# Recurrence blocks back inside the hidden products, and a changed start: a wider table of decays, zero products sooner, and the second batch's inputs on ScalarE's queue

## The chip, the cores and the metric

The kernel runs on one core of a Trainium2 chip. The core has five engines with a queue each: TensorE (PE, matmuls; PEld is its weight load), VectorE (DVE), ScalarE (ACT), GpSimd (POOL) and SyncE (SP, which only issues transfers here). The metric is the device time of one execution in microseconds. Before the change the median of three runs is 671.96 us (670.41 to 673.58).

## The reference

Two stages. The first is a retention recurrence over 4 batches, 8 heads, 768 tokens and 64 dimensions, with a decay `gamma` per head:

```
state = gamma * state + k_t (outer) v_t
y_t   = (1/8) * q_t @ state
```

The second takes the 3072 x 512 matrix of all `y` (tokens by heads and dimensions) through a two-layer network: `h = x @ w_in` (512 to 2048), `g = max(0.01 h, h)`, `out = g @ w_out` (2048 to 512). The weights arrive as 64-bit floats and are turned into 32-bit floats on the core.

## The kernel before

**The recurrence in chunks.** The 768 tokens are six chunks (c = 0 to 5) of 128. In a chunk, a batch b needs four groups of small matmuls: `score` (keys times queries, 16 matmuls on 64 x 64 tiles of the array), `reads` (queries times the state carried in, 8 on 64 x 64 tiles), `values` (masked scores times decayed values, 8 on 128 x 64 tiles) and `state` (keys times values, 8 on 128 x 64 tiles). Between `score` and `values`, DVE multiplies the scores by a triangular mask (`masked`), and some engine multiplies the values by decays (`decay_v`: on GpSimd unless another is given). After `values` and `state`, DVE takes the tokens into `x` (`tokens_taken`) and updates the state (`state_taken`, two operations of 256 columns).

**The network.** It goes by chunk and by unit u (four units of 512 hidden columns). Each matrix product is done with seven half-size products in place of eight, `seven`: M1, M6, M5, M4, M2, M7, M3 in the order `ORDER`, each of four 128 x 128 by 128 x 256 matmuls per unit (recorded as 8), into the PSUM banks A, B, C, D (M1 and M2 share A, M6 and M7 share B, M5 and M3 share C). `hidden` (L530 to L563) makes `g` from `x` and the differences `t` of `x`; `output` (L565 to L619) makes the result from `g` and its differences `gd`. Behind each product the engines take its bank: ScalarE copies M1 and M5 out (L540, L546), DVE does the sums (L446), ScalarE the leaky step (L535, L550). M1 and M2 use only `x`; M6, M5 and M4 use `t`. The order `FIRST` does M2 straight after M1.

**Order.** There is no scheduler: each engine does its instructions in the order in which the program emits them. `seven` is a generator that yields after each product, and `run(steps, at)` emits other work at chosen steps. Chunks 0 and 1 go together, unit by unit, while weights are still converted; chunks 2 to 5 follow one by one, with units in pairs: hidden, hidden, output of the pair.

**Visits.** From chunk 2 on the recurrence work of a later chunk stands behind an output (L843 to L858). A `visit(c, b, following)` (L310 to L344) handles batches b and b+1: scores of the first following batch into two single banks of tag "ff" (`score_apart`), reads, values, scores of the second following batch, states; DVE's masks, tokens, the four differences of `x` if the chunk is then complete, state updates; and then the loads of the next chunk's inputs. The queries and keys of batches 2 and 3 are loaded into the tile of an output not in use (`ahead`, L270). After a visit that completes a chunk, the first hidden goes in the order `FIRST`. Exceptions: in the last output of chunk 0, the scores of batches 0 and 1 of chunk 2 stand after M1 and a visit without following after M4 (L836); in the last output of chunk 1 the scores of batches 2 and 3 stand after M2 (L840).

**The start.** SyncE issues the transfers in order: queries and keys of batch 0 (`load_qk`), values of batch 0 (`load_v`), the same of batch 1, two weight pieces, and so on (L672 to L687). ScalarE issues one, the table of decays (L671): 8 rows of 780 columns. DVE sets the mask and then 256 columns of zeros (L688, L700). PE does seven products of zeros (`keep_busy`, L703), scores of batch 0, three matmuls that spread the decays over all partitions (L717 to L723, contraction over the table's 8 rows), scores of batch 1, values of batch 0, and so on until the first direct product of weights (`direct`, L522 at L739). DVE copies gains and carry `gk`, `gc` out of PSUM (L722) and multiplies batch 0's values (L726); ScalarE copies `gq` (L725). Each weight piece needs three ScalarE steps (`powers`, L419 to L422) and three DVE steps (`mantissas_upper` L431, `mantissas_rest` L440 and L442).

Of the kernel before, what the change touches and what calls it, by code (L numbers as in the profile page):

```python
# [18 lines left out]
C = 128  # L19
# [4 lines left out]
def kernel(  # L24
# [104 lines left out]

    def load_qk(c, b):  # L130
        nc.sync.dma_start(out=heads[c, b][0], in_=qk[c, b])

    def load_v(c, b):
        nc.sync.dma_start(out=heads[c, b][1][:, 1], in_=kv[c, b][:, 1])

# [31 lines left out]

    turn = [0]

    def new_am(c, b):  # L170

        i = turn[0]
        turn[0] = (i + 1) % (3 if (c, b) >= (2, 2) else 2)
        if i < 2:
            return work.tile([128, 2, HP, C], FP32, tag=f"am{i}", name=f"am_{c}_{b}")
        place = new_t(1, f"am_{c}_{b}").rearrange("p i k n -> p (i k n)")[:, 0 : 2 * HP * C]
        return place.rearrange("p (j a t) -> p j a t", j=2, a=HP)

    def new_t(c, name):
        return work.tile([128, 3, 2, N], FP32, tag=f"t{int(c == 1)}", name=name)  # L180

    def new_o(c, name="o"):
        return work.tile([128, 4, 2, N], FP32, tag=f"o{int(c > 0)}", name=f"{name}_{c}")

    def masked(c, b):
        am = new_am(c, b)
        nc.vector.tensor_tensor(
            out=am.rearrange("p j a t -> p (j a) t"),
            in0=scores[c, b].rearrange("p j a t -> p (j a) t"),
            in1=mask.unsqueeze(1).to_broadcast([128, H, C]), op=ALU.mult)  # L190
        scores[c, b] = am
# [25 lines left out]
    def state(c, b):  # L217
        y = heads[c, b][1]
        sp = for_state(sums_at[c, b])
        for a in range(HP) if c < NC - 1 else ():  # L220
            sums_of(sp, y, a)
# [47 lines left out]

    def ahead(c, b):  # L270


        if c >= NC:
            return
        if b < 2:
            x = work.tile([128, 2, HP, C], FP32, tag="qk", bufs=AHEAD, name=f"qk_{c}_{b}")
        else:
            if b == 2:
                room[c] = new_o(0).rearrange("p i k n -> p (i k n)")
            x = room[c][:, ds((b - 2) * 2 * HP * C, 2 * HP * C)]  # L280
            x = x.rearrange("p (s a t) -> p s a t", s=2, a=HP)
        heads[c, b] = [x, None]
        load_qk(c, b)

    def load_kv(c, b):
        y = work.tile([128, 2, H, D], FP32, tag="kv", bufs=AHEAD, name=f"kv_{c}_{b}")
        heads[c, b][1] = y
        nc.sync.dma_start(out=y, in_=kv[c, b])

    room = {}  # L290

    def score_apart(c, b):

        x = heads[c, b][0]
        ps = scores[c, b] = [psum.tile([128, HP, C], FP32, tag="ff", bufs=4, name=f"ap{j}_{c}_{b}")
                             for j in range(2)]
        for a in range(HP):
            for u in range(2):
                for j in range(2):
                    nc.tensor.matmul(ps[j][ts(u, 64), a, :], lhsT=x[ts(j, 64), 1, a, ts(u, 64)],  # L300
                                     rhs=x[ts(j, 64), 0, a, :])

    def masked_apart(c, b):
        am = new_am(c, b)
        for j, ps in enumerate(scores[c, b]):
            nc.vector.tensor_tensor(out=am[:, j], in0=ps,
                                    in1=mask.unsqueeze(1).to_broadcast([128, HP, C]), op=ALU.mult)
        scores[c, b] = am

    def visit(c, b, following=None, complete=False):  # L310

        bs, xb = (b, b + 1), xs[c][0]
        more = [(following[0], following[1] + i) for i in range(2)] if following else [None, None]
        early, late = more

        def do(f, at):
            if at is not None:
                f(*at)

        do(score_apart, early)  # L320
        for i in bs:
            reads(c, i)
        do(masked_apart, early)
        for i in bs:
            values(c, i)
        do(score_apart, late)
        for i in bs:
            state(c, i)
        do(masked_apart, late)
        for i in bs:  # L330
            tokens_taken(c, i, xb)
        if complete:
            if xs[c][1] is None:
                xs[c][1] = new_t(c, f"t_{c}")
            differences(*xs[c])
        for i in bs:
            state_taken(c, i)
        for i in bs:
            if c + 1 < NC:
                ahead(c + 1, i)  # L340
        for at in more:
            do(load_kv, at)
        for at in more:
            do(decay_v, at)  # L344

# [129 lines left out]
    ORDER = (0, 1, 2, 3, 4, 5, 6)  # L475
    FIRST = (0, 4, 1, 2, 3, 5, 6)

# [147 lines left out]
    def new_x(c):  # L625
        x = tile_x(c)
        return [x, new_t(c, f"t_{c}") if c < 3 else None]

# [15 lines left out]
    def scored(c, b):  # L644
# [4 lines left out]
        return do  # L649

    def differ(c):
        return lambda: differences(*xs[c])
# [11 lines left out]
    place_for(0, 1)  # L664
    place_for(0, 2, new_o(0, "in"))
    place_for(0, 3, new_o(1, "in"))
    words = tile_x("words").rearrange("p i k n -> p (i k n)")[:, 0 : 2 * W]
    xs = {0: new_x(0)}
    x, t = xs[0]
    rows = t[0:H, 1:3].rearrange("p i k n -> p (i k n)")[:, 0 : decay.shape[1]]  # L670
    nc.scalar.dma_start(out=rows, in_=decay)  # L671
    load_qk(0, 0)  # L672
    load_v(0, 0)
    load_qk(0, 1)
    load_v(0, 1)
    load_piece(0)
# [21 lines left out]

    nothing = t[:, 0, 0, :].bitcast(BF16)
    nc.vector.memset(t[:, 0, 0, :], 0.0)  # L700
    idle = psum.tile([128, 2, N], FP32, tag="ff", bufs=4, name="idle")

    def keep_busy(n):  # L703
        for _ in range(n):
            nc.tensor.matmul(idle.rearrange("p i n -> p (i n)"), lhsT=nothing[:, 0:128],
                             rhs=nothing, start=True, stop=True, skip_group_check=True)

# [6 lines left out]
    by_head, ones, place, g_q, g_c = (rows[:, i:j] for i, j in zip(ends, ends[1:]))  # L714
    keep_busy(7)
    score(0, 0)
# [4 lines left out]
    masked(0, 0)  # L721
    nc.vector.tensor_copy(out=dec[:, n_gq:], in_=tables[:, 0, 0 : H + HP])  # L722
    nc.tensor.matmul(spread.rearrange("p i n -> p (i n)"), lhsT=place, rhs=g_q, start=True,  # L723
                     stop=True, skip_group_check=True)
    nc.scalar.copy(out=dec[:, 0:n_gq], in_=spread.rearrange("p i n -> p (i n)"))  # L725
    decay_v(0, 0, nc.vector)  # L726
    score(0, 1)
# [75 lines left out]
    scored_later(3)  # L803
    later = hidden(1, 0, x1, t1, *parts[1][1:], order=FIRST)
    next(later)
# [14 lines left out]
    for u in range(NU):  # L820
        for c in range(2) if u > 0 else ():
            if c == 0:
                parts = []
            parts.append(new_g(c, u))
            run(hidden(c, u, *xs[c], *parts[c][1:]), rounds(1, 3))
        for c in range(2):
            if u == 0:
                os[c] = new_o(c)
            at = rounds(1, 4) if u < NU - 1 else {}
            if u == 0 and c == 0:  # L830
                put(at, s2=[differ(0)])
            if u == NU - 1 and NC > 2:
                if c == 0:
                    xs[2] = new_x(2)
                if c == 0:
                    at = {0: [scored(2, 0), scored(2, 1)], 3: [lambda: visit(2, 0)]}  # L836
                else:
                    at = {1: [lambda: ahead(2, 2), lambda: ahead(2, 3)],
                          2: [lambda: load_kv(2, 2), lambda: load_kv(2, 3)],
                          4: [scored(2, 2), scored(2, 3)]}  # L840
            run(output(c, os[c], [parts[c]], u == 0, u == NU - 1), at)

    if NC > 2:  # L843
        visit(2, 2, (3, 0) if NC > 3 else None, complete=True)
    for c in range(2, NC):
        os[c] = new_o(c)
        for p in range(NU // 2):
            pair = []
            for u in (2 * p, 2 * p + 1):
                pair.append(new_g(c, u))  # L850
                run(hidden(c, u, *xs[c], *pair[-1][1:], order=ORDER if u else FIRST), {})
            run(output(c, os[c], pair, p == 0, p == NU // 2 - 1), {})

            if c + 1 < NC and p == 0:
                xs[c + 1] = new_x(c + 1)
                visit(c + 1, 0, (c + 1, 2))
            elif c + 1 < NC and p == NU // 2 - 1:
                visit(c + 1, 2, (c + 2, 0) if c + 2 < NC else None, complete=True)  # L858

# [4 lines left out]
def _decay(H, D):  # L864
# [11 lines left out]
    place = np.concatenate([place, np.zeros((H - 2, place.shape[1]))])  # L876
    return np.concatenate([np.exp(-lg[:, None] * t[None, :]), np.eye(H), place],
                          axis=1).astype(np.float32)

# [62 lines left out]
```

## Time and profile before

| What | Value |
|---|---|
| median of three runs | 671.96 us |
| the profiled execution's own time | 671.96 us |
| its span, first to last instruction | 669.9 us |
| mean granted TensorE clock | 0.997 |
| PE busy | 661.1 us (99%) |
| DVE, ACT, POOL busy | 369.3, 176.2, 18.9 us |
| bytes read and written | 41.97 MB, 6.29 MB |

How to read the profile's lines. A line of a timeline gives start and duration in us, the engine, the line in the code, the operation, what it writes and reads by the program's names, shapes and how many records are merged; in brackets the idle time before it and what ended it. Durations of matmuls overlap: what a group costs is read from start to start. A line of waits gives who waited for whom, the total in us, how often, and the longest. A line by windows gives a stretch, its length, the busy share of each engine with the number of instructions, the granted TensorE clock (1.00 is full), the share of the transfer engines in use and the rate in GB/s.

### The profile page before, as it was taken

What the parts mean: (1) busy time and instruction counts of PE and PEld (TensorE: products, weight loads), DVE (VectorE), ACT (ScalarE), POOL (GpSimd) and SP (SyncE); (2) the same over time, 40 slices, a digit from 0 to 9 for tenths busy, and PEclk for the clock granted to TensorE, in tenths of its full rate; (3) what the DMA queues carried; (4) which work ended last, traced back from release to release, by engine and by line L of the source; (5) the groups of instructions that cost most, each with busy time, mean ns of one, the idle gap of its engine ahead of it and who ended that gap; (6) DMA issues with size and microseconds to landing.
All of it is one profiled execution on the core that took longest, in us unless ns stands there. A gap on an engine that the chain in (4) does not pass through costs nothing.

```text
span 669.9 us, 10441 instructions
## 1 busy us (share of the span) xinstructions
PE 661.1 (99%) x4503; PEld 573.7 (86%) x4505; DVE 369.3 (55%) x582; ACT 176.2 (26%) x322; POOL 18.9 (3%) x22
## 2 busy tenths in 40 slices
PE   8999999999999999999999999999999999999998
PEld 5888888888888888888888888888888888888886
DVE  4789969889888673344436413536433443541342
ACT  4764555264261002202102211300210210221210
POOL 0000000000000020001001001001000100000000
PEclk8999999999999999999999999999999999999999
DMA  8920311312322540020022003005001001000001
GB/s 329 393 100 32 125 64 66 124 64 103 117 79 90 221 179 1 0 100 28 1 90 100 1 0 127 1 6 184 1 0 52 13 1 64 0 1 1 0 1 63
DMA packets 15757, 48.92 MB, mean 73 GB/s; under 512 B 1752, under 2 KB 2008, under 8 KB 15712
## 3 DMA queue, kind: packets, MB, share of 16 engines
q1 hardware_dynamic: 15696, 48.24, 19.8%
q8 instruction: 35, 0.57, 0.3%
q14 instruction: 10, 0.08, 0.0%
q10 hardware_dynamic: 16, 0.02, 0.0%
HBM read 41.97 MB, written 6.29 MB: 72 GB/s over the span
## 4 chain that ended last, share of the span: by engine, by line
PE 98%; DMA 1%; DVE 0%; ACT 0%; issue 0%; SPq 0%; DVEq 0%
PE B_o L500 12%; PE A_o L500 12%; PE C_o L500 12%; PE A_h L500 12%; PE B_h L500 12%; PE C_h L500 12%; PE D_o L500 6%; PE D_h L500 6%; PE yp L210 4%; PE d L522 2%; PE ap L300 2%; PE ap L165 2%; PE yp L201 1%; PE yp L225 1%; DMA qk<-in_qk_dram 1%; ACT m L540 0%
## 5 line engine op out<-in xcount | busy, mean ns | idle before, releaser
L500 PE MATMUL A_h<-x,w 128*128 128x256 f32 x368 | 88.2, 382 | 2.7 <-ACT m L540 2.7
L500 PEld LDWEIGHTS A_h<-x,w 128*128 128x128 f32 x368 | 68.9, 190 | 14.1 <-ACT m L540 4.3
L500 PE MATMUL A_o<-g,w 128*128 128x256 f32 x288 | 68.0, 379 | 0.0
L446 DVE TENSOR_TENSOR m<-m,B_h 128x512 f32<-128x512 f32 x23 | 15.8, 686 | 90.6 <-PE B_h L500 90.6
L500 PEld LDWEIGHTS A_o<-g,w 128*128 128x128 f32 x288 | 54.7, 190 | 7.4
L535 ACT ACTIVATE g<-g 128x512 f32<-128x512 f32 x69 | 42.0, 630 | 72.7 <-DVE g L446 72.7
L540 ACT COPY m<-A_h 128x512 f32<-128x512 f32 x23 | 13.5, 586 | 176.6 <-PE A_h L500 156.3
L446 DVE TENSOR_TENSOR m<-m,B_o 128x512 f32<-128x512 f32 x16 | 11.0, 685 | 64.3 <-PE B_o L500 64.3
L500 PE MATMUL B_h<-t,w 128*128 128x256 f32 x184 | 43.5, 379 | 0.0
L500 PE MATMUL D_h<-t,w 128*128 128x256 f32 x184 | 43.5, 379 | 0.0
L500 PE MATMUL C_h<-t,w 128*128 128x256 f32 x184 | 43.5, 379 | 0.0
L500 PE MATMUL B_h<-x,w 128*128 128x256 f32 x184 | 43.5, 379 | 0.0
L500 PE MATMUL C_h<-x,w 128*128 128x256 f32 x184 | 43.5, 379 | 0.0
L500 PEld LDWEIGHTS B_h<-t,w 128*128 128x128 f32 x184 | 35.0, 190 | 4.8
L500 PEld LDWEIGHTS D_h<-t,w 128*128 128x128 f32 x184 | 35.0, 190 | 4.8
L500 PEld LDWEIGHTS B_h<-x,w 128*128 128x128 f32 x184 | 35.0, 190 | 4.8
L500 PEld LDWEIGHTS C_h<-x,w 128*128 128x128 f32 x184 | 35.0, 190 | 4.8
L500 PEld LDWEIGHTS C_h<-t,w 128*128 128x128 f32 x184 | 35.0, 190 | 4.8
L449 DVE TENSOR_TENSOR gd<-g,gd 128x512 f32<-128x512 f32 x48 | 33.2, 692 | 1.7
L500 PE MATMUL D_o<-gd,w 128*128 128x256 f32 x144 | 34.0, 379 | 0.0
L500 PE MATMUL C_o<-g,w 128*128 128x256 f32 x144 | 34.0, 379 | 0.0
L500 PE MATMUL B_o<-gd,w 128*128 128x256 f32 x144 | 34.0, 379 | 0.0
(122 smaller groups left out, 995.3 us busy)
## 6 DMA issues: line engine op xcount, KB each, us to landing
raw<-in_weights_dram SPq DMA_DIRECT2D x31, 512.0 KB, 4.1
kv<-in_kv_dram SPq DMA_DIRECT2D x17, 512.0 KB, 4.9
out_dram<-o SPq DMA_DIRECT2D x23, 256.0 KB, 2.2
qk<-in_qk_dram SPq DMA_DIRECT2D x11, 512.0 KB, 3.6
o<-in_qk_dram SPq DMA_DIRECT2D x8, 512.0 KB, 3.4
in<-in_qk_dram SPq DMA_DIRECT2D x5, 512.0 KB, 8.6
in<-in_kv_dram SPq DMA_DIRECT2D x3, 512.0 KB, 7.6
kv<-in_kv_dram SPq DMA_DIRECT2D x4, 256.0 KB, 7.0
```

The lines of the kernel that those rows point to most:

```text
L165: nc.tensor.matmul(ps[ts(u, 64), j, a, :], lhsT=x[ts(j, 64), 1, a, ts(u, 64)], rhs=x[ts(j, 64), 0, a, :])
L201: nc.tensor.matmul(ps[ts(i, 64), j, m, :], lhsT=st[b][ts(j, 64), a, :], rhs=x[ts(j, 64), 0, a, :], start=(m == 0), stop=False, skip_group_ ...
L210: nc.tensor.matmul(ps[ts(i, 64), j, m, :], lhsT=y[:, 1, 2 * a + j, :], rhs=am[:, j, a, :], start=(c == 0 and m == 0), stop=True, skip_grou ...
L225: nc.tensor.matmul(sp[ts(j, 64), a, :], lhsT=y[:, 0, 2 * a + j, :], rhs=y[:, 1, 2 * a + j, :], start=start, stop=True, skip_group_check=True)
L300: nc.tensor.matmul(ps[j][ts(u, 64), a, :], lhsT=x[ts(j, 64), 1, a, ts(u, 64)], rhs=x[ts(j, 64), 0, a, :])
L446: nc.vector.tensor_tensor(out=out, in0=a, in1=b, op=ALU.add)
L449: nc.vector.tensor_tensor(out=out, in0=a, in1=b, op=ALU.subtract)
L500: nc.tensor.matmul(half, lhsT=block(w, sa)[:, k, ts(i, 128)], rhs=rhs[:, k, :], start=(first and (i == 0 or split) and n == 0 and k == 0), ...
L522: nc.tensor.matmul(banks[r][:, i, :], lhsT=block(2 * u, r + 2 * kh)[:, k, ts(i, 128)], rhs=x[:, 2 * kh + th, k, :], start=(step == 0 and i ...
L535: nc.scalar.activation(g[:, i], g[:, i], AF.Prelu, alpha=0.01)
L540: nc.scalar.copy(out=got["m1"], in_=ps)
```

## The change

The visits go. From chunk 2 on the recurrence is emitted inside other products: the scores of two batches of chunk c+1 after M6 of the hidden product of units 0 and 2 of chunk c, and their reads, values and states after M2 of the same (`read`, `stage_y`); the differences of `x` after M6 of the chunk's last output. In the last outputs of chunks 0 and 1 the scores stand after M1 and the reads after M4; chunk 2's differences after M2 of chunk 1's. All hidden products of chunks 2 to 5 go in `ORDER`. Queries and keys of later chunks go to the two "qk" tiles, loaded when the tile before is read; scores always use the two-bank tiles of tag "att". The tags of the tiles `am`, `t` and `o` become plain rotations of two.

At the start: the table of decays has 32 rows (24 of them zeros), GpSimd sets the rows of the other partitions to zero, and the three spreading matmuls contract over 128 partitions. Zeros for `keep_busy` are 64 columns, set by DVE ahead of the mask, and read repeatedly; eight such products instead of seven. Batch 1's queries, keys and values are issued by ScalarE. Gains and carry are copied by ScalarE, and batch 0's values are multiplied by GpSimd.

```
-        nc.sync.dma_start(out=heads[c, b][0], in_=qk[c, b])
+    def load_qk(c, b, queue=nc.sync):
+        queue.dma_start(out=heads[c, b][0], in_=qk[c, b])
+    def load_v(c, b, queue=nc.sync):
+        queue.dma_start(out=heads[c, b][1][:, 1], in_=kv[c, b][:, 1])
...
-        am = new_am(c, b)
+        am = work.tile([128, 2, HP, C], FP32, tag="am", bufs=2, name=f"am_{c}_{b}")
...
-    def visit(c, b, following=None, complete=False):
...
+    def stage_y(c, bs, xb):
+        products(c, bs)
+        for b in bs:
+            taken(c, b, xb)
+            n = c * B + b + AHEAD
+            if c > 1 and n < NC * B:
+                load(*divmod(n, B))
...
+    def read(c, *bs):
+        return lambda: stage_y(c, bs, xs[c][0])
...
-    rows = t[0:H, 1:3].rearrange("p i k n -> p (i k n)")[:, 0 : decay.shape[1]]
-    nc.scalar.dma_start(out=rows, in_=decay)
+    rows = t[:, 1:3].rearrange("p i k n -> p (i k n)")[:, 0 : decay.shape[1]]
+    n_rows = decay.shape[0]
+    nc.scalar.dma_start(out=rows[0:n_rows], in_=decay)
+    nc.gpsimd.memset(rows[n_rows:64], 0.0)
+    nc.gpsimd.memset(rows[64:128], 0.0)
+    nothing = t[:, 0, 0, 0:64].bitcast(BF16)
+    nc.vector.memset(t[:, 0, 0, 0:64], 0.0)
     load_qk(0, 0)
     load_v(0, 0)
-    load_qk(0, 1)
-    load_v(0, 1)
+    load_qk(0, 1, nc.scalar)
+    load_v(0, 1, nc.scalar)
...
-    nothing = t[:, 0, 0, :].bitcast(BF16)
-    nc.vector.memset(t[:, 0, 0, :], 0.0)
...
-            nc.tensor.matmul(idle.rearrange("p i n -> p (i n)"), lhsT=nothing[:, 0:128],
-                             rhs=nothing, start=True, stop=True, skip_group_check=True)
+            nc.tensor.matmul(idle.rearrange("p i (two n) -> p (i two) n", two=2), lhsT=nothing,
+                             rhs=nothing.unsqueeze(1).to_broadcast([128, 4, 128]),
+                             start=True, stop=True, skip_group_check=True)
...
-    keep_busy(7)
+    keep_busy(8)
...
-    nc.vector.tensor_copy(out=dec[:, n_gq:], in_=tables[:, 0, 0 : H + HP])
+    nc.scalar.copy(out=dec[:, n_gq:], in_=tables[:, 0, 0 : H + HP])
...
-    decay_v(0, 0, nc.vector)
+    decay_v(0, 0)
...
-                if c == 0:
-                    at = {0: [scored(2, 0), scored(2, 1)], 3: [lambda: visit(2, 0)]}
-                else:
-                    at = {1: [lambda: ahead(2, 2), lambda: ahead(2, 3)],
-                          2: [lambda: load_kv(2, 2), lambda: load_kv(2, 3)],
-                          4: [scored(2, 2), scored(2, 3)]}
+                at = {0: [scored(2, 2 * c), scored(2, 2 * c + 1)],
+                      3: [read(2, 2 * c, 2 * c + 1)]}
+                if c == 1:
+                    put(at, s4=[differ(2)])
...
-    if NC > 2:
-        visit(2, 2, (3, 0) if NC > 3 else None, complete=True)
...
-                run(hidden(c, u, *xs[c], *pair[-1][1:], order=ORDER if u else FIRST), {})
-            run(output(c, os[c], pair, p == 0, p == NU // 2 - 1), {})
...
+                at = {}
+                if more and u == 2 * p:
+                    at = {1: [scored(c + 1, u), scored(c + 1, u + 1)],
+                          4: [read(c + 1, u, u + 1)]}
+                run(hidden(c, u, *xs[c], *pair[-1][1:]), at)
+            at = {1: [differ(c + 1)]} if p == 1 and more else {}
+            run(output(c, os[c], pair, p == 0, p == NU // 2 - 1), at)
...
+    rows = np.concatenate([np.exp(-lg[:, None] * t[None, :]), np.eye(H), place], axis=1)
+    return np.concatenate([rows, np.zeros((32 - H, rows.shape[1]))]).astype(np.float32)
```

## The prediction

> **What bounds the kernel now.** I read the page first: the shares by engine and the chain that ended last. The first line below is the engines, the second the chain by engine.
>
> ```profile
> PE 661.1 (99%) x4503; PEld 573.7 (86%) x4505; DVE 369.3 (55%) x582; ACT 176.2 (26%) x322; POOL 18.9 (3%) x22
> PE 98%; DMA 1%; DVE 0%; ACT 0%; issue 0%; SPq 0%; DVEq 0%
> ```
>
> TensorE (PE) is nearly always at work, so a time can only come from three places: its idle stretches, the cost of its matmuls in another order, and its clock. The list of waits from 15.4 us to the end gives PE's idle time: two entries, 2.7 and 0.4 us. The larger one:
>
> ```profile
> PE A_h L500 <- ACT m L540: 2.7, 4, 0.7
> ```
>
> Four times 0.68 us, each in the first hidden product of a chunk. PE's timeline around one of them (start, duration, line, operation; records of one kind are merged, and start to start is what a group costs) shows a visit, and then the hidden products in the order FIRST:
>
> ```profile
> 346.34 1.03 PE L500 MATMUL C_o<-g,last_s 128*128 128x256 f32 x4
> 347.30 1.10 PE L300 MATMUL ap<-qk 64*64 64x128 f32 x32
> 348.22 1.05 PE L201 MATMUL yp<-o,states 64*64 64x128 f32 x32
> 349.20 1.97 PE L210 MATMUL yp<-am,kv 128*64 128x128 f32 x32
> 351.10 1.10 PE L300 MATMUL ap<-qk 64*64 64x128 f32 x32
> 352.14 1.15 PE L225 MATMUL yp<-kv 128*64 128x64 f32 x32
> 353.22 1.99 PE L500 MATMUL A_h<-x,w 128*128 128x256 f32 x8
> 355.89 1.99 PE L500 MATMUL A_h<-x,w 128*128 128x256 f32 x8 [0.68 <-ACT m L540]
> ```
>
> The two A_h groups are M1 and M2. Both go to bank A, so M2 waits until ScalarE has copied M1 out: 2.67 us from M1 to M2, where a product costs 1.73 us inside a dense run (C_o from 210.44 to 212.17). The same trace also holds the other arrangement, once, in the last output of chunk 0, which the change leaves alone:
>
> ```profile
> 206.71 1.98 PE L165 MATMUL ap<-qk 64*64 64x128 f32 x64
> 208.61 1.99 PE L500 MATMUL B_o<-gd,last 128*128 128x256 f32 x8
> 210.44 1.89 PE L500 MATMUL C_o<-gd,last 128*128 128x256 f32 x8
> 212.17 1.89 PE L500 MATMUL D_o<-gd,last 128*128 128x256 f32 x8
> 213.99 1.10 PE L201 MATMUL yp<-qk,states 64*64 64x128 f32 x32
> 216.82 1.10 PE L225 MATMUL yp<-kv 128*64 128x64 f32 x32
> 217.85 1.99 PE L500 MATMUL A_o<-g,last 128*128 128x256 f32 x8
> ```
>
> Two scores together 1.90 us, the read block 3.86 us, and no wait. Last the head, by PE's timeline and by slices of 1 us (the figure after POOL's count is the granted clock, then DMA share and GB/s):
>
> ```profile
> 8.18 1.67 PE L165 MATMUL ap<-qk 64*64 64x128 f32 x32 [0.73 <-DMA qk<-in_qk_dram]
> 9.79 1.97 PE L210 MATMUL yp<-am,kv 128*64 128x128 f32 x16
> 15.41 0.92 PE L522 MATMUL d<-x,w 128*128 128x256 f32 x3 [0.40 <-DVE w L442]
> 9.00:10.00 1.00, 1.00 (x19) 0.67 (x14) 0.10 (x1) 0.00 (x0) 0.99 (x1) 0.50 1.03 422
> ```
>
> From 15.41 us on PE is dense. Before it lies the head, and in it the clock is at half: the slices 8 to 9 and 11 to 12 (means 0.78 and 0.51) put that from about 8.56 to 11.98 us. The batch 1 score and batch 0 values ran in it at 1.61 and 1.97 us, against 1.03 and 1.03 for such groups at 13.16 and 25.09.
>
> **The recurrence blocks.** Each block is priced with what it adds at its edges: the product before it takes 1.82 instead of 1.73 (+0.09 or 0.10), the one behind it 1.83 (+0.10).
> Removed. Behind outputs there are seven visits. Without FIRST behind them (at 292.83 and 402.70): 5.92 + 0.19 = 6.11 and 6.12. With FIRST (237.42, 347.30, 457.17): 5.92 + 0.10 + 0.94 (2.67 − 1.73) + 0.10 = 7.06 each. The last two do less: 4.84 + 0.19 = 5.03 (512.58) and 2.93 + 0.10 + 0.94 + 0.10 = 4.07 (565.96). Sum 42.5. With the scored pair at 231.87 (1.90 + 0.20 = 2.1) that is 44.6 us.
> Added. A scored pair costs 2.1 and a read block 3.86 + 0.20 = 4.06, so 6.16 for a pair of batches. Five pairs (the second of chunk 2, all of chunks 3 and 4): 30.8. The two of chunk 5 have no state matmuls (read block 2.93 + 0.19 = 3.12): 2 × 5.2 = 10.4. Sum 41.2.
> Difference −3.4 us: −3.4 for four times 0.84 of FIRST, +1.1 for six more blocks at 0.19, −1.1 because scores now stand together instead of split by other tile shapes. The bounds: −4.3 (edges free, as six times 0.15 would vanish) and 0 (each stall comes back elsewhere). I take −3.3, near the sum, as both arrangements stand in one trace.
>
> What could be late next, from M1 of a hidden at 0. After M6 (3.5 us) VectorE (DVE) does u2 0.69 and two masks 2.35 (two L187 in a row) and is done near 7.2; the read block begins near 10.8, so 3.6 us are spare. Behind it DVE has the tokens and states of two batches, 2.8 us (217.50 to 220.29), ahead of M7's three sums of 0.61; bank B is free 3.1 us after the block, and the next hidden asks for it at 5.4. M6's t now comes from differences one or two products after the previous output's M6, so M6 needs no FIRST. The tightest place is chunk 2's second pair: by the same durations bank B is free near 242.6 and asked for at 243.1. If that misses, PE loses some 0.3 us, once. The key and value loads go out when a read block ends, ahead of the output's stores on SyncE's queue; their landings (medians 3.6 and 4.9 us) stand against 7 us at the tightest (chunk 2) and over 20 elsewhere. GpSimd's multiplies (1.08 us each) hide in the same gap; uncovered they cost 1.1 us a batch.
>
> **The head.** Five edits act together.
> (1) Batch 1's two transfers leave SyncE's queue for ScalarE's and run beside batch 0's. On SyncE they took 0.89 and 0.43 us to issue; ScalarE pays that ahead of its table load (1.28), idle until 7.49 anyway. Batch 0's scores input landed at 4.58 us; it now shares the engines, and lands between 4.6 (nothing lost) and 8.84 (everything of batch 1 first: the landing of its values before). I take 5.6: estimated from the 324 GB/s of slice 2 to 3, half of it from about 2.3 us. Batch 1's scores input then lands near 7.1 instead of 8.14, weight piece 0 between 9.4 and 10.1.
> The skill page "DMA: Bandwidth & Descriptors", section "Issuing engines are not separate DMA queues", says that transfers issued by several engines interleave on the same 16 engines and only issue time is saved. By it alone the head would gain no bytes and a late batch 0 would speak against the change; the total would be 668.6.
> (2) The zero products: the 256-column memset (0.27) and the mask's (0.17) no longer lie ahead of them, so they start near 1.1 instead of 1.39; eight at 0.43 end at 4.55, as before. Worth nothing by themselves: the input follows.
> (3) The table: 8 rows become 128, by 32 rows of DMA (100 KB instead of 24, 0.25 us at 400 GB/s) and two GpSimd memsets (780 columns; bounds 0.3 us by the mask's select and 1.6 by 1.08 us for 512 columns of two inputs), done long before 5.9. The tables keep their 1.57 us (5.88 to 7.45).
> (4) Gains and carry go through ScalarE (0.2 us), batch 0's multiply through GpSimd (1.08): 1.3 us beside DVE's mask (1.22) instead of 0.85 us on DVE behind it. Both multiplies in a row on GpSimd end near 9.6, before batch 1's mask.
> (5) PE then: scores 5.6 to 6.6, tables to 8.15, score 1 to 9.2, values 0 to 10.25, no idle. If the clock holds: mask 1 9.35 to 10.55, tokens 0 to 11.2, piece 0's first step (0.42) to 11.6; values 1 10.6 to 11.65, tokens 1 to 12.4, piece 0's two steps to 13.9. The first d product starts near 13.9 instead of 15.41: −1.5, of which I take −1.3 for handoffs. Later needs (piece 2 at 18.6 for PE at 19.8; the last keys by 21.0 for 23.1) leave it standing.
> If the clock halves again near 8.5, the durations of before hold from 8.15 on and the gain is 0. The bounds: −2.5 (piece 0 landed at 10.12, three ScalarE steps 2.0 and one DVE step 0.69 follow: 12.85) and +1.75 (batch 0's input at 8.84).
>
> Does it hold? Half-width matmuls alone don't take the clock: 5.9 us of them from 292.83 ran in a stretch at 1.00. The 3.4 us before the drop (as long as the drop itself) hold 0.73 us of idle and 1.57 us of 8-row matmuls. The change takes both. That rows count is my guess; no row shows it.
> The page "TensorE: Matmul & The Clock Gate", section "What's actually happening", halves the clock after an idle window of about 3.4 us. By that rule 0.73 us of idle wouldn't have halved it; the trace shows it halved, so the trace decides. By the page the drop isn't cured by rows, and the sum would be 668.7.
>
> **Sum.** The profiled execution took 671.96 us, span 669.9 and 2.06 around it, and equals the median of the three runs. 671.96 − 3.3 − 1.3 = 667.4.
>
> **Rivals.**
> A: clock halves again. For it: 0.45 us idle ahead of batch 0's scores remains. Against: the 8-row matmuls are gone. 671.96 − 3.3 = 668.7.
> B: the stall only moves. M6 waits for differences or a bank in the place of M2, 0.68 each four times, 2.7. For it: the 0.5 us margin in chunk 2. Against: the margins above. 671.96 − 3.3 + 2.7 − 1.3 = 670.1.
> C: slower. The masks inside the hidden products hold the read block, since its two PSUM pairs are those of the scores. At 3.6 us spare, DVE must be 5 us late in each of six blocks: then 6 × 1.4 = 8.4 us, and 671.96 − 4.6 + 8.4 = 675.8. It outweighs the gain from 4.4 us late. For it: the masks now stand before M7's sums. Against: DVE is busy 23 of 55 us there (42%), and nothing waited at 213.99.
>
> **How the numbers follow.** Forecast 0.53, A 0.25, B 0.12, C 0.10. The forecast's own range is 666.0 to 668.6, from the head's bounds and 0.3 us of the blocks. The range 665.6 to 670.6 takes in A and B, and below the head's −2.5; C is left out. About 0.5% (3.4 us, 668.6) is what a measurement can tell from no change. Faster: 0.9 of the forecast and half of A, 0.61; slower 0.10; same 0.29.
>
> **What would show it.** No PE wait on ScalarE's m copy in chunks 2 to 5; scored blocks near 1.90 and read blocks near 3.86 within hidden products, without waits; clock 1.00 from 8 to 12 us; first d product near 13.9; the first scores not before 5. Wrong if a read block or M6 waits over 0.5 us, or if batch 0's input lands after 6.5.

## The result, and the profile after

The kernel after takes 666.84 us (median of six executions, 666.78 to 667.28) against 670.50 us for the kernel before beside it (670.00 to 673.58): the ratio is 0.9937, with a 95% interval of 0.9918 to 0.9955, so 3.7 us or 0.6% faster. The profiled execution took 667.28 us, with a span of 665.6 us and 1.68 around it.

One thing has to be said ahead of the comparison. The profiled execution of before, 671.96 us, on which the prediction was built, was not a typical one. In 56 later executions of the same kernel, whose mean clocks were recorded one by one, 8 had 0.997 (671.1 to 671.9 us), 6 took 673.6 to 673.8 us at a recorded 1.000, and the rest lay around 670.5 us. The half clock between 8.56 and 11.98 us that the trace of before shows was an event of that execution; 3.42 us at half in 669.9 is what makes a mean of 0.997. No execution near 673.6 us was profiled, so what happened in those isn't known.

The page of the kernel after, engines and chain:

```profile
PE 659.2 (99%) x4506; PEld 572.5 (86%) x4506; DVE 372.7 (56%) x568; ACT 175.9 (26%) x323; POOL 22.4 (3%) x25
PE 98%; DMA 1%; DVE 0%; POOL 0%; ACTq 0%; issue 0%; DVEq 0%
```

TensorE is the bound as before. Its list of waits over the whole span (who waited for whom: total, times, longest):

```profile
PE ap L165 <- DMA qk<-in_qk_dram: 1.2, 1, 1.2
PE idle L629 <- DVE t L597: 1.1, 1, 1.1
PE yp L193 <- POOL kv L147: 0.5, 1, 0.5
PE d L436 <- DVE w L357: 0.4, 1, 0.4
```

All four lie in the first 15 us. The four waits of A_h for ScalarE's copy (2.7 us) are gone, and no wait took their place. PE's timeline in the first hidden of chunk 2, with chunk 3's recurrence inside it:

```profile
240.36 1.89 PE L414 MATMUL A_h<-x,w 128*128 128x256 f32 x8
242.08 1.89 PE L414 MATMUL B_h<-t,w 128*128 128x256 f32 x8
243.90 1.98 PE L165 MATMUL ap<-qk 64*64 64x128 f32 x64
245.81 1.99 PE L414 MATMUL C_h<-t,w 128*128 128x256 f32 x8
247.64 1.89 PE L414 MATMUL D_h<-t,w 128*128 128x256 f32 x8
249.37 1.89 PE L414 MATMUL A_h<-x,w 128*128 128x256 f32 x8
251.19 1.10 PE L184 MATMUL yp<-qk,states 64*64 64x128 f32 x32
252.22 1.97 PE L193 MATMUL yp<-am,kv 128*64 128x128 f32 x32
254.02 1.10 PE L208 MATMUL yp<-kv 128*64 128x64 f32 x32
255.05 1.99 PE L414 MATMUL B_h<-x,w 128*128 128x256 f32 x8
```

The two scores take 1.91 us, the read block 3.86 (251.19 to 255.05), as in the one sample of before. M6 (B_h at 242.08) follows M1 by 1.72 us, so the tightest place cost nothing. From the first direct product to the end of the span it is 665.6 − 14.38 = 651.2 us, where before had 669.9 − 15.41 = 654.5: 3.3 us from the blocks.

The head of the kernel after, by its timeline (PE's groups and GpSimd's second multiply):

```profile
5.58 1.10 PE L165 MATMUL ap<-qk 64*64 64x128 f32 x32 [1.24 <-DMA qk<-in_qk_dram]
8.12 1.10 PE L165 MATMUL ap<-qk 64*64 64x128 f32 x32
9.15 1.09 PE L193 MATMUL yp<-am,kv 128*64 128x128 f32 x16
10.00 1.04 POOL L147 TENSOR_TENSOR kv<-kv,dec 128x512 f32<-128x512 f32 x1 [1.45 <-DMA kv<-in_kv_dram]
11.10 1.09 PE L193 MATMUL yp<-am,kv 128*64 128x128 f32 x16 [0.53 <-POOL kv L147]
14.38 2.99 PE L436 MATMUL d<-x,w 128*128 128x256 f32 x12 [0.38 <-DVE w L357]
```

And the slice of 9 to 10 us, in which before had a granted clock of 0.50 (the figure behind POOL's count):

```profile
9.00:10.00 1.00, 1.00 (x25) 0.85 (x16) 0.71 (x1) 0.77 (x2) 0.00 (x0) 1.00 1.03 412
```

The pace is full and the first direct product starts at 14.38 instead of 15.41 us. But batch 1's values, on ScalarE's queue beside two weight pieces, landed 8.2 us after their issue at 1.73, at 9.93 us (8.84 before): GpSimd waits for them, and PE for GpSimd.

### The profile page after: what moved, and what is told of

Same layout as the page of the kernel before. It is cut to its first block, busy times and chain, and to the rows that moved or that the text cites. A ratio compares the mean times of both kernels' runs of the same rounds, so it can differ in the third digit from the quotient of the medians.

```text
span 665.6 us, 10410 instructions
## 1 busy us (share of the span) xinstructions
PE 659.2 (99%) x4506; PEld 572.5 (86%) x4506; DVE 372.7 (56%) x568; ACT 175.9 (26%) x323; POOL 22.4 (3%) x25
## 4 chain that ended last, share of the span: by engine, by line
PE 98%; DMA 1%; DVE 0%; POOL 0%; ACTq 0%; issue 0%; DVEq 0%
PE B_o L414 13%; PE A_o L414 13%; PE C_o L414 12%; PE B_h L414 12%; PE C_h L414 12%; PE A_h L414 12%; PE D_o L414 6%; PE D_h L414 6%; PE yp L193 3%; PE ap L165 3%; PE d L436 2%; PE yp L184 2%; DMA kv<-in_kv_dram 1%; PE yp L208 1%; PE sums L208 0%; POOL kv L147 0%
## 5 line engine op out<-in xcount | busy, mean ns | idle before, releaser
L238 DVE TENSOR_TENSOR x<-yp,dec 128x512 f32<-128x512 f32 x24 | 16.4, 688 | 50.0 <-PE yp L208 35.1
L364 DVE TENSOR_TENSOR gd<-g,gd 128x512 f32<-128x512 f32 x48 | 36.2, 754 | 1.7
L147 POOL TENSOR_TENSOR kv<-kv,dec 128x512 f32<-128x512 f32 x18 | 20.5, 1137 | 456.8 <-DMA kv<-in_kv_dram 440.8
L170 DVE TENSOR_TENSOR am<-ap,mask 128x1024 f32<-128x1024 f32 x24 | 28.5, 1219 | 12.1 <-PE ap L165 12.1
```

The lines of the kernel that those rows point to most:

```text
L147: engine.tensor_tensor(out=v, in0=v, in1=gk.unsqueeze(2).to_broadcast([128, H, D]), op=ALU.mult)
L170: nc.vector.tensor_tensor(out=am.rearrange("p j a t -> p (j a) t"), in0=scores[c, b].rearrange("p j a t -> p (j a) t"), in1=mask.unsqueeze ...
L238: nc.vector.tensor_tensor(out=blocks, in0=ps[:, :, 0 : HP // 2, :], in1=gq, op=ALU.mult)
L364: nc.vector.tensor_tensor(out=out, in0=a, in1=b, op=ALU.subtract)
```

## The experiments

Three groups ran, each beside the kernel before: the first four below (670.55 us for the kernel before), the scores at two places with the last three (670.46), and the other four (670.63). The kernel after itself took 666.84 us the first time and 666.62 in the group of the last three, so a difference of 0.25 us or less between groups says nothing.

**The start of before under the new blocks.**

```
-    load_qk(0, 1, nc.scalar)
-    load_v(0, 1, nc.scalar)
+    load_qk(0, 1)
+    load_v(0, 1)
...
-    keep_busy(8)
+    keep_busy(7)
...
-    decay_v(0, 0)
+    decay_v(0, 0, nc.vector)
```

(The table, the zeros and the copy of gains and carry go back likewise.)

> The kernel after with the start of before: table of 8 rows, one queue for both batches, seven zero products behind the mask's memset, gains copied and batch 0 multiplied by VectorE. Theory (two separate gains, blocks 3.3 us and head 1.0 us): 3.3 us under the kernel before, the first direct product near 15.4 us from the span's start, clock at half from about 8.5 to 12 us, and from that product to the end 651.2 us as in the kernel after (654.5 before). Rival (the gain sits in the start): within 1 us of before. If the clock's drop comes in some executions and not in others, the executions of this kernel split into two groups: those with a mean clock of 0.997 about 1.5 us longer than those with 1.000.

Measured 667.25 us, ratio 0.9951 (0.9939 to 0.9964): 3.3 us under the kernel before, without the new start. The five executions: 667.96 and 667.83 us at a mean clock of 0.997, the others 666.70 to 667.25 at 0.999 or 1.000, so a group of two appeared, 0.9 us apart rather than 1.5. In the profiled one the clock held, and the old start was no slower than the new (PE's timeline):

```profile
7.71 1.10 PE L165 MATMUL ap<-qk 64*64 64x128 f32 x32
8.75 1.09 PE L193 MATMUL yp<-am,kv 128*64 128x128 f32 x16
14.28 2.97 PE L436 MATMUL d<-x,w 128*128 128x256 f32 x13
```

Batch 1's scores start at 7.71 us, and the first direct product at 14.28, against 14.38 in the profile of after. The expected 15.4 us failed: it had been taken from the one disturbed trace. From the first direct product to the end it is 665.2 − 14.28 = 650.9 us, as with the new start (651.2).

**The table's rows.**

```
-    rows = t[:, 1:3].rearrange("p i k n -> p (i k n)")[:, 0 : decay.shape[1]]
-    n_rows = decay.shape[0]
-    nc.scalar.dma_start(out=rows[0:n_rows], in_=decay)
-    nc.gpsimd.memset(rows[n_rows:64], 0.0)
-    nc.gpsimd.memset(rows[64:128], 0.0)
+    rows = t[0:H, 1:3].rearrange("p i k n -> p (i k n)")[:, 0 : decay.shape[1]]
+    nc.scalar.dma_start(out=rows, in_=decay)
```

(The table itself has 8 rows again.)

> The kernel after with the table contracted over its 8 rows again and no rows of zeros: no GpSimd memsets, 24 KB of table. Theory (rows count for the clock): the clock halves near 8.5 us for some 3.4 us, the scores of batch 1 take 1.6 us, the first direct product starts near 15.4 us instead of 14.4, 1 us slower than the kernel after. Rival (only idle time counts, and the idle ahead of batch 0's scores fell into another stretch): clock 1.00 throughout, first direct product at 14.4, the same time as the kernel after within 0.3 us.

Measured 667.03 us (666.86 to 667.10), the mean clock 1.000 in all four executions, the first direct product at 13.96 us. The rows of zeros are worth nothing that shows, and eight rows alone don't take the clock: the theory of the rows fails, at least under the early zeros.

**One queue for both batches.**

```
-    load_qk(0, 1, nc.scalar)
-    load_v(0, 1, nc.scalar)
+    load_qk(0, 1)
+    load_v(0, 1)
```

> The kernel after with batch 1's queries, keys and values issued by SyncE again, behind batch 0's. Theory (rows count): batch 0's scores start at 4.6 us, batch 1's near 8.1 after some 0.7 us of idle, clock 1.00 all the same; batch 1's values land near 8.9 instead of 9.9, so the values of batch 1 don't wait for GpSimd, and the first direct product starts near 13.9, 0.5 us before that of the kernel after: 0.5 us faster than it. Rival (idle time takes the clock): half clock from about 8.5, first direct product near 15.4, 1 us slower than the kernel after.

Measured 666.48 us (666.34 to 666.85), 4.1 us under the kernel before beside it where the kernel after is 3.7 and 3.8 under: 0.2 to 0.4 faster, hardly more than two groups can tell. PE has no wait on GpSimd; its only wait behind the zero products is 0.8 us ahead of batch 2's scores. The first direct product stands at 14.12, not 13.9. The clock stayed at 1.00, and the idle time expected ahead of batch 1's scores didn't come: batch 0's ran partly at half pace (1.98 us) and ended later.

**FIRST alone.**

```
-                run(hidden(c, u, *xs[c], *pair[-1][1:], order=ORDER if u else FIRST), {})
+                run(hidden(c, u, *xs[c], *pair[-1][1:], order=ORDER), {})
```

> The kernel before with ORDER in place of FIRST for the first hidden of chunks 2 to 5. Theory (the stall belongs to the place of the differences, not to the order): M6 waits for the second difference, 0.8 to 1.2 us each in place of 0.68 us at M2; four times, 0 to 2 us slower than before, none of the 3.3 us won. Rival (FIRST alone costs the stall): four times 0.84, 3.4 us faster than before.

Measured 671.61 us, ratio 1.0016 (1.0003 to 1.0029): 1.1 us slower than before. The wait moves from M2 to M6, and grows (the wait list, then PE's timeline from M1):

```profile
PE B_h L500 <- DVE t L449: 3.8, 4, 1.1
```

```profile
241.53 1.99 PE L500 MATMUL A_h<-x,w 128*128 128x256 f32 x8
244.66 1.97 PE L500 MATMUL B_h<-t,w 128*128 128x256 f32 x8 [1.13 <-DVE t L449]
```

3.8 − 2.7 = 1.1 us, the whole difference. So FIRST was the smaller of two stalls while the differences stood behind the visit. In the kernel after the differences of chunk 2 into t are done at 240.97 us, ahead of its M6 at 242.08, and the wait is gone; no run has them early with the visits kept.

**The read block straight behind the scores.**

```
-                    at = {1: [scored(c + 1, u), scored(c + 1, u + 1)],
-                          4: [read(c + 1, u, u + 1)]}
+                    at = {1: [scored(c + 1, u), scored(c + 1, u + 1), read(c + 1, u, u + 1)]}
```

> The kernel after with the read block straight behind the two scores in the hidden products of chunks 2 to 4, in place of three products later. Theory (the three products between them cover the two masks on VectorE): PE waits for the masks, about 1.8 us in each of six blocks, less 0.19 for the edge that goes: 9 to 11 us slower than the kernel after, 676 to 678. Rival (the masks are no matter, and the distance is): 1 us faster than the kernel after by the edges saved.

Measured 673.29 us, 6.5 us over the kernel after, which is less than expected. PE's timeline:

```profile
243.35 1.98 PE L165 MATMUL ap<-qk 64*64 64x128 f32 x64
245.80 0.67 PE L184 MATMUL yp<-qk,states 64*64 64x128 f32 x16 [0.47 <-DVE am L170]
246.93 0.67 PE L184 MATMUL yp<-qk,states 64*64 64x128 f32 x16 [0.46 <-DVE am L170]
247.53 1.97 PE L193 MATMUL yp<-am,kv 128*64 128x128 f32 x32
250.35 1.99 PE L414 MATMUL C_h<-t,w 128*128 128x256 f32 x8
```

Each read waits for its own mask, 0.93 us idle for the two. From the start of the scores to C_h it is 7.00 us, where scores and read block apart take 1.91 + 3.86 = 5.77: 1.23 more, six times 7.4, less 1.1 for six edges, 6.3. The expectation had let everything wait for the second mask; the masks overlap the first reads. So the masks do hold a read block where nothing stands between, and three products between are enough.

**The scores at two places.**

```
-                    at = {1: [scored(c + 1, u), scored(c + 1, u + 1)],
+                    at = {0: [scored(c + 1, u)], 1: [scored(c + 1, u + 1)],
                           4: [read(c + 1, u, u + 1)]}
```

> The kernel after with the two scores of a pair at two places in the hidden products of chunks 2 to 4: the first behind M1, the second behind M6. Theory (every block pays 0.19 us at its edges): six more blocks, 1.1 us slower than the kernel after, 667.9. Rival (edges cost nothing): the same within 0.3 us.

Measured 668.91 us, 2.3 us over the kernel after beside it (666.62), twice what was expected. PE's timeline, with no waits:

```profile
239.95 1.89 PE L414 MATMUL A_h<-x,w 128*128 128x256 f32 x8
241.77 1.10 PE L165 MATMUL ap<-qk 64*64 64x128 f32 x32
242.81 2.00 PE L414 MATMUL B_h<-t,w 128*128 128x256 f32 x8
244.73 1.10 PE L165 MATMUL ap<-qk 64*64 64x128 f32 x32
245.76 2.00 PE L414 MATMUL C_h<-t,w 128*128 128x256 f32 x8
247.59 1.89 PE L414 MATMUL D_h<-t,w 128*128 128x256 f32 x8
```

From A_h to D_h 7.64 us against 7.28 in the kernel after: 0.36 for one more block, six times 2.2 us. The expected 1.1 us had only the edge on the wide products, which is 0.20 here (three of them take 5.57 us against 5.37). The other 0.16 is on the scores: a block of its own takes 1.03 to 1.04, not half of 1.91.

**Batch 1's values on SyncE, its queries and keys on ScalarE.**

```
     load_qk(0, 1, nc.scalar)
-    load_v(0, 1, nc.scalar)
+    load_v(0, 1)
```

> The kernel after with only batch 1's values issued by SyncE again, ahead of the weight pieces; its queries and keys stay with ScalarE. Theory (the second queue costs because batch 1's values share the engines with two weight pieces and land late): they land before 9.0 us instead of 9.9, the values products of batch 1 no longer wait for GpSimd (0.53 us in the kernel after), 0.3 us faster than the kernel after, as with everything on one queue. Rival (the second queue costs because batch 0's scores start late): no faster than the kernel after, the first scores still after 5 us.

Measured 666.15 us (666.10 to 666.81), ratio 0.9926 (0.9901 to 0.9951), the quickest version here: 4.5 us under the kernel before beside it. The values landed at about 7.7 us (issued at 1.7, 6.0 us to landing), and PE's timeline has no wait for GpSimd:

```profile
4.59 1.25 PE L165 MATMUL ap<-qk 64*64 64x128 f32 x32
9.84 1.09 PE L193 MATMUL yp<-am,kv 128*64 128x128 f32 x16
13.44 3.62 PE L436 MATMUL d<-x,w 128*128 128x256 f32 x16
```

So the values landing behind the weight pieces was what the second queue cost. The gain over the kernel after, 0.6 to 0.8 us between groups, is more than the 0.3 expected; batch 0's scores start here at 4.59 too, but they did so in the second profile of the kernel after (4.58), so that part varies from one execution to the next.

**Two zero products fewer ahead of the first direct product.**

```
-    load_qk(0, 1, nc.scalar)
-    load_v(0, 1, nc.scalar)
+    load_qk(0, 1)
+    load_v(0, 1)
...
-    keep_busy(3)
+    keep_busy(1)
```

> The kernel after with batch 1 on SyncE's queue and one zero product instead of three ahead of the first direct product. Theory (with one queue that product starts behind the zero products at 14.1 us, where its weights are ready at 13.8): 0.2 to 0.3 us faster than with one queue alone. Rival (what follows is bound by the weights' conversion on VectorE): the same within 0.1 us.

Measured 666.84 us (666.22 to 666.91): no gain over one queue alone (666.48), so the expected 0.2 to 0.3 us failed. PE's timeline has its last wait ahead of the first direct product (13.99 us):

```profile
12.73 1.10 PE L165 MATMUL ap<-o_in 64*64 64x128 f32 x32 [0.97 <-DMA o_in<-in_qk_dram]
```

Batch 2's queries and keys land near 12.7 us in this execution. Neither theory named that transfer.

**The zeros of before under the new start.**

```
-    nothing = t[:, 0, 0, 0:64].bitcast(BF16)
-    nc.vector.memset(t[:, 0, 0, 0:64], 0.0)
...
+    nothing = t[:, 0, 0, :].bitcast(BF16)
+    nc.vector.memset(t[:, 0, 0, :], 0.0)
...
-    keep_busy(8)
+    keep_busy(7)
```

> The kernel after with the zeros of before: 256 columns set behind the mask, seven zero products from 1.4 us. Theory (earlier zero products keep the clock): some of the executions have a mean clock of 0.997, 1 us longer than the others, as with the whole start of before. Rival (the table's rows or the queue keep it): mean clock 0.999 or 1.000 in all, and the time of the kernel after within 0.3 us.

Measured 666.69 us in the median, and one of six executions at 668.73. That one was the profiled one; PE's timeline:

```profile
1.40 3.17 PE L629 MATMUL idle<-t 128*128 128x512 bf16 x7 [1.40 <-DVE t L624]
7.42 2.05 PE L648 MATMUL spread<-t 128*128 128x512 f32 x2
9.40 1.68 PE L165 MATMUL ap<-qk 64*64 64x128 f32 x32
```

Its slice of 9 to 10 us:

```profile
9.00:10.00 1.00, 1.00 (x13) 0.60 (x16) 0.00 (x0) 0.49 (x2) 0.60 (x1) 1.00 1.07 434
```

The array ran at half pace up to about 11 us: the spread took 2.05 us where 1.10 is usual, the scores 1.68 where 1.10. The granted clock of the slice says 1.00 all the same, so here the column doesn't show it, and the durations do. The mean clock was 0.999, not the 0.997 expected: this is another event than the one in the trace of before, a late start of full pace.

The same edit on the quickest version:

> The quickest arrangement so far (batch 1's values on SyncE's queue, queries and keys on ScalarE's) with the zeros of before: 256 columns behind the mask, seven products from 1.4 us. Theory (earlier zeros keep the pace): one in four executions 1 us or more above the others, the others at 666.1 to 666.4. Rival: none, all within 0.7 us.

Measured 666.39 us in the median, one of six executions at 668.65, the rest 665.98 to 666.47. The slow one is again the profiled one, and has the same shape: spread from 7.34 us in 2.05, batch 1's scores from 9.33 in 1.69, full pace behind them.

The opposite edit, on the kernel before:

```
+    nothing = t[:, 0, 0, 0:64].bitcast(BF16)
+    nc.vector.memset(t[:, 0, 0, 0:64], 0.0)
...
-    keep_busy(7)
+    keep_busy(8)
```

> The kernel before with one edit of the start alone: 64 columns of zeros ahead of the mask, eight zero products from 1.06 us. Theory (earlier zero products keep the array at full pace through the head): no execution over 671 us and none with a mean clock of 0.997; the median as before, 670.2 to 670.6. Rival (rows or queue keep it): one in four executions between 671.3 and 673.8, as with the kernel before.

Measured 670.48 us against 670.46 for the kernel before: the same (0.9997, 0.9988 to 1.0006). But none of its 12 executions lay over 670.92 us, while of 23 of the kernel before beside it four had a mean clock of 0.997 (671.1 to 671.9) and one took 673.60.

The kernel after again, unchanged:

> The kernel after unchanged, beside the other two on the same chip: 666.7 to 667.3 us, no execution with a mean clock of 0.997, and 0.5 to 0.7 us over the arrangement with batch 1's values on SyncE's queue.

Measured 666.62 us (666.53 to 666.70), no execution with 0.997; 0.2 us over the version beside it with the values on SyncE and the late zeros, where 0.5 to 0.7 had been expected. How much of the 0.6 to 0.8 us of the quickest version lasts beside it under the early zeros isn't settled by this pair.

Counted over all kernels by when the zero products start, an event being a mean clock of 0.997 or a time two us or more above the kernel's median (only the two late starts above were profiled among them, so the other cases go by clock and time alone): from 1.4 us (seven of them), 21 of 83 executions had an event (kernel before 14 of 56, old start 2 of 5, order alone 3 of 10, late zeros 1 of 6 and 1 of 6); from 1.06 us (eight), 1 of 57 had (the read block at once, 675.45 us at 0.997).

## Why the prediction was right, and where it was not

**The blocks, −3.3 us.** Right: 3.27 us between the traces (654.49 to 651.22), and 3.3 from the run that has the new blocks with the old start. The working by start-to-start times of blocks that the trace of before held held up; the bounds weren't needed. Two traces in which the clock held, the kernel before with early zeros (668.3 − 14.06 = 654.2) and the old start (650.9), differ by 3.3 as well. The sum was right, but its split into three terms was not: by its own figures FIRST cost 0.95 a visit (7.06 less 6.11), 3.8 in four where it says 3.4, and scores that are split 0.16 a visit (5.92 less 1.90 and 3.86), 0.8 in five where it says 1.1. The run with the scores at two places shows both edges, 0.20 on the wide products and 0.16 on parted scores.

**What could be late next.** Right that nothing would be: no PE wait behind 15 us. The margin named as the tightest, 0.5 us for bank B at 242.6 and 243.1, was near zero in the trace (M7's sum ran from 241.48 to 242.16, M6 began at 242.08), and cost nothing.

**The head, −1.3 us.** Between the two profiled executions it was −1.03 (15.41 to 14.38), and the time around the span fell by another 0.4 (2.06 to 1.68), for which the prediction had no term, so the sum from 671.96 to 667.4 met the profiled 667.28. Against the medians the head is worth some 0.4 us, 3.7 in all less 3.3; but two of the five executions of the old start had a mean clock of 0.997, and the median of the other three, 666.98 us, leaves 0.1 to 0.4 (666.84 and 666.62), near the noise. The traces agree: where the clock held, the start of before reached its first direct product at 13.84 us (the order alone) and 14.28 (the old start), the new one at 14.38, 13.71 (the kernel after again) and 13.82 (the read block at once). The step that failed is that the durations of one profiled execution were taken for those of every execution. A mean clock of 0.997 came in 8 of 56, and the median of the three runs had coincided with such an execution. So it is partly luck that the sum came within 0.6 us of the median: it began 1.5 us too high (671.96 against 670.5) and took off 1.3 us for a head whose gain was nearly all this one event.

**The cause of the half clock.** Wrong, as far as counts can show it. The prediction took the eight-row matmuls and the idle time for it, and wrote of the earlier zero products that they are worth nothing by themselves. With eight rows and the early zeros none of 16 executions had the lower clock, so 128 rows aren't needed; and the one execution at 0.997 under early zeros (675.45 us) had 128 rows, so they don't prevent it. Nor did 0.65 us of idle just ahead of 8.12 us take the clock in the run with two zero products fewer. With the zeros of before under the new start, late starts of full pace came (1 of 6, twice); with the early zeros alone the kernel before had no event in 12. So the zero products count, by 1 in 57 against 21 in 83. Not settled is whether the rows do something under the late zeros: there 12 of 71 executions with eight rows had 0.997, and none of 12 with 128 rows, which is too few to tell. Whether it is the 0.34 us sooner or the eighth product isn't separated either, and what makes an execution fall into one event or the other is open.

The page "TensorE: Matmul & The Clock Gate" of the Trainium skill, section "What's actually happening", says that the clock is released after a busy window of about 3.4 us that doesn't begin with the kernel. The seven products last 3.17 us and the eight 3.3 to 3.6, but the trace of the late zeros doesn't fit that rule as it stands: PE has no wait from 1.40 to 12 us, and the scores at 9.40 us, 8 us later and so more than two such windows (an estimate by the page's figure), still began at half pace. No run here shows the window itself.

**The second queue.** Half right. Batch 0's scores moved to 5.58 us, as taken (5.6). Batch 1's queries and keys landed at 7.96, not near 7.1, and its values at 9.93, which the step about GpSimd ("end near 9.6") passed over: the transfer that became late was the one issued last on the new queue, beside two weight pieces. The page "DMA: Bandwidth & Descriptors", section "Issuing engines are not separate DMA queues", was quoted against this part, and the runs agree in that the second queue by itself gained nothing: with one queue for both batches the kernel is 0.2 to 0.4 us faster, if that is more than noise.

**Rivals.** A (half clock again, 668.7) didn't occur in the 12 executions of the kernel after; with the old start two of five had the lower clock, at 667.9 us, and the two executions near 668.7 with late zeros were the other event. B and C didn't occur, though the order alone and the read block at once show that both mechanisms exist where the distance is taken away. Two small slips in the prediction's numbers changed nothing: 0.9 of the forecast and half of A make 0.60, not 0.61, and the upper end of the forecast's own range, 668.6, is a head worth nothing and not the bound of +1.75, which gives 670.4.

**Open.** The time around the span is 1.95 us with the old blocks and 1.7 to 1.8 with the new (670.55 − 668.6, 666.78 − 665.1); some 0.2 us of the gain is there, and no run tells why.

## What to carry to other kernels

A stall at a boundary is not cured by choosing which instruction waits; give the late producer its place a stage earlier, and put work between the halves of a dependent pair that is at least as long as what lies between them on the other engine. Where a short phase sets part of the time, look at it in several executions before a price is read from it, by durations and not only by the clock column. A transfer that is moved to a second queue can come later there (9.93 instead of 8.84 us here): ask which transfer is late then, and put the small one that is needed first ahead of the large ones.

## What the runs showed of the hardware that was not expected

The granted clock and the pace can differ: in the run with late zeros the record says 1.00 from 1 to 11 us while one 512-column product in two passes took 2.05 us instead of 1.10. In that run PE had no wait from 1.40 to 12 us, and full pace came only behind 9.40 us. One more block of 16 matmuls on 64 x 64 tiles, parted from its neighbour and put between 128 x 128 products, cost 0.36 us. And 0.34 us of earlier zero products with one more of them left the median of the kernel before where it was (670.48 against 670.46 us), while none of its 12 executions had an event, against 5 of the 23 beside it.
